# Laying a kernel's spare path ahead of its main path, and regrouping its mixer: one change of a tuned transformer block

## The chip, the cores and the metric

The kernel runs on one core of a Trainium2 chip. The metric is the device time of one execution in microseconds (us), lower is better; the figure quoted for a kernel is the median of its runs. Five engines appear: PE (matmul; PEld is its weight load), ACT (activations), DVE (vector work), POOL (general work), SP (used here only to issue DMAs).

## The reference, cut to what matters

```python
mod = (silu(c) @ w_mod).reshape(1, 6, 1, 640)        # c: (1, 640), w_mod: (640, 3840)
sa, ca, ga, sb, cb, gb = (mod[:, i] for i in range(6))
h = layernorm(x) * (1 + ca) + sa                     # x: (2048, 640), bfloat16
q = h @ wq                                           # 32 heads of 128
o = softmax(q @ k_cache.T * 128**-0.5) @ v_cache     # caches: 32 x 2048 x 128
x = x + ga * (o @ wo)                                # modulation 2 is ga
h = layernorm(x) * (1 + cb) + sb
# the mixer: u = gelu(layernorm(h) @ w1); four groups of 160 channels are shifted by
# 1, -1, 2, -2 rows; x1 = h + u_shifted @ w2; then an MLP of width 1728
x = x + gb * (x1 + gelu(layernorm(x1) @ w3) @ w4)
```

Of the kernel before, what the change touches and what calls it, by code (L numbers as in the profile page):

```python
# [6 lines left out]
ACT = mybir.ActivationFunctionType  # L7
# [33 lines left out]
class Plan:  # L41
# [3 lines left out]
    ENG = ("PE", "ACT", "DVE", "POOL", "SP")  # L45

# [115 lines left out]
    def emit(self, nc, es, ndma, redo, flag):  # L162
        hint = {}
# [67 lines left out]
        def body(e):  # L231
            def f(eng):
                for i, o in enumerate(self.seq[e]):
                    if e == "PE" and i == len(self.seq[e]) - 300:
                        hint[e] = eng.mark_branch_hint_location()
                    for sem, v in waits[o].items():
                        eng.wait_ge(sem, v)
                    ins = o.fn(eng)
                    if o.dma:
                        ins.then_inc(o.sem, 16)  # L240
                    elif o.needed:
                        ins.then_inc(o.sem, 1)
                eng.wait_ge(self.flag_op.sem, self.flag_op.semval)
                eng.load(redo[eng.engine], flag[0:1, 0:1])
                for sem in dsem.get(e, ()):
                    if fin.get(sem, 0) > know[e].get(sem, 0):
                        eng.wait_ge(sem, fin[sem])
            return f

        block = es.enter_context(nc.Block())  # L250
        block.tensor(body("PE"))
        block.scalar(body("ACT"))
        block.vector(body("DVE"))
        block.gpsimd(body("POOL"))
        block.sync(body("SP"))
        return hint


def fast_path(nc, es, flag, A_x, A_k_cache, A_v_cache, A_wq, A_wo, B_w1, B_w2, B_w3, B_w4, c, w_mod, out):
# [72 lines left out]
    us = [T() for _ in range(NC)]  # L332
# [16 lines left out]
    W12 = [T(), T()]  # L349
    w_half = [W12_t[:, i * KT * D:(i + 1) * KT * D].rearrange("p (k n) -> p k n", k=KT) for i in range(2)]  # L350
# [23 lines left out]
    def dma(eng, fn, kb, reads, writes, prio, need=()):  # L374
        return P.op(eng, fn, {"SP": 480, "ACT": 480, "POOL": 1000}[eng], reads, writes, prio, dma=True, kb=kb, need=need)
# [9 lines left out]
    for i in range(NKV):  # L385
        P.op("POOL", lambda e, i=i: e.memset(V_ap[i][:, :, 128:130], 1.0), 200, (), (V[i],), -297 + i)
# [16 lines left out]
    x0 = load_x2(0, -301) + load_x2(2, -301, eng="ACT")  # L403
# [29 lines left out]
    P.op("DVE", lambda e: e.tensor_copy(s_bc.ap, c_f.ap.unsqueeze(2).to_broadcast([128, KT, 128])), 800, (c_f,), (s_bc,), 0.5)  # L433
    spin(50, -298)
    for k in range(KT):
        def mcol(e, k=k):
            for j in range(2 * KT):
                ins = e.matmul(mc[:, j:j + 1], wm_ap[:, k, j * 128:(j + 1) * 128], s_bf[:, k:k + 1],
                               start=(k == 0 and j == 0), stop=(k == KT - 1), skip_group_check=True)
                if k < KT - 1:  # L440
                    dummy(e, 1)
            return ins
        P.op("PE", mcol, 2 * KT * 120, (wm[k], s_bf, ones), (mc,) + ((warm,) if k < KT - 1 else ()), -290 + k, accum=True)
    spin(12, -281)
# [83 lines left out]
    def ln1(ch, prio):  # L528
        g = ln_slot()
        xs = x0 if ch == 0 else load_x2(4 * ch, XP[ch], from_slot(XS[ch])) + load_x2(4 * ch + 2, XP[ch], from_slot(XS[ch]))  # L530
        for a in (0, 2):
            for i in (a, a + 1):
                ln_stats(xs[i].ap, (xs[i],), g, i, prio, 0.0 if ch == 0 else 2000.0)
            rstd_act(g, a, a + 2, prio - 100)
# [3 lines left out]
        if ch == 0:  # L538
# [5 lines left out]
            for i in range(4):  # L544
# [4 lines left out]
                P.op("PE", tr, 330, (xn[i], ident), (hp[0], hp[1], hq, hp[4]), -280 + i, accum=True)  # L549
                spin(6 if i < 3 else 10, -279.5 + i)  # L550
# [18 lines left out]
    def load_k(h, prio, gate=(), need=()):  # L569
        b = h % NKV  # L570
        for i in range(4):
            dmaT(lambda e, i=i: e.dma_start_transpose(K_ap[b][:, i * 512:(i + 1) * 512].unsqueeze(1), A_k_cache[0, h, i * 512:(i + 1) * 512, :]),
                 128, gate, (K[b][i],), prio + 0.01 * i, need)
# [5 lines left out]
    def load_wq(g, a, b, prio, need=()):  # L579
        dma("SP", lambda e: e.dma_start(wq_t[g % 2][:, :, a * 128:b * 128],  # L580
                                        A_wq[:, (g * HG + a) * 128:(g * HG + b) * 128].rearrange("(k p) d -> p k d", p=128)),
            160 * (b - a), (), tuple(wq[g % 2][a:b]), prio, need)
# [8 lines left out]
    load_k(0, -296)  # L591
    load_v(0, -290, "ACT", gate=(wm[3],))
    ln1(0, -280)

    def load_head(h):
# [3 lines left out]
        load_k(h, pr, need=from_slot(n))  # L599
        load_v(h, pr + 1, need=from_slot(n + 1))  # L600
# [6 lines left out]
    load_wq(0, 1, HG, -295)  # L607
# [4 lines left out]


    MS = 17
    for n, p in enumerate((2, 4, 3, 5)):
        dma("SP", lambda e, n=n, p=p: e.dma_start(w_half[n % 2], w_mod[:, p * D:(p + 1) * D].rearrange("(k p) n -> p k n", p=128)),
            800, (), (W12[n % 2],) + (tuple(wm) if n < 2 else ()), MS * NP - 30 + n, from_slot((MS + 2 * n) * NP - 20))
        for hf in range(2):
            m = Tile(pool="M")
            sl = slice(hf * HD, (hf + 1) * HD)  # L620
            for k in range(KT):
                i = (n * 2 + hf) * KT + k
                P.op("PE", lambda e, m=m, sl=sl, k=k, n=n: e.matmul(m[:, 0:HD], s_bc[:, k, :], w_half[n % 2][:, k, sl], start=(k == 0), stop=(k == KT - 1)),
                     MM(HD), (s_bc, W12[n % 2]), (m,), NP * (MS + i // KT) + 4 + i % KT + 0.65, accum=True)
            P.op("DVE", lambda e, m=m, p=p, hf=hf: e.tensor_scalar_add(out=mod[p][hf].ap, in0=m[:, 0:HD], scalar1=1.0 if p == 4 else 0.0),
                 490, (m,), (mod[p][hf],), NP * MS - 60)

# [1045 lines left out]
```

## The kernel before: what the change and the argument touch

The program is a list of operations, each with tiles that it reads and writes and a priority. A scheduler fixes the order on each engine ahead of time, and `emit` writes the five instruction streams with semaphore waits. Attention is 128 "steps": 32 heads in eight groups of four, by four chunks of 512 queries. A step has eight pairs of score matmuls, eight exponentials of 1024 columns on ACT, and the matmuls with V. `TAIL` is the order of the pieces of mixer and MLP: A = `w1`, B = `w2`, C = `w3`, D = `w4`, WO = the last output projection.

The main path skips the maximum of the softmax. At the end it computes a flag from the row sums; if the flag is set, a general path computes everything again. **With these inputs the general path never runs**, but its code lies in the program.

```python
# emit, before: one block, a body for each engine; a barrier closes the block
def body(e):
    def f(eng):
        for i, o in enumerate(self.seq[e]):
            if e == "PE" and i == len(self.seq[e]) - 300:
                hint[e] = eng.mark_branch_hint_location()
            ...                                    # waits, the instruction, its increments
        eng.wait_ge(self.flag_op.sem, self.flag_op.semval)
        eng.load(redo[eng.engine], flag[0:1, 0:1])
        ...
# launch, before: then each engine jumps, over the general path, to "done"
for e, eng in nc.engines.items():
    br = eng.br_cmp(redo[e], 0, comp_op="IS_EQ", on_true="done", on_false="general")
    if eng is nc.tensor:
        br.branch_hint(hint["PE"])
with nc.body("general"):
    general_path(nc, ...)
    nc.br("done")
nc.switch_bb("done")
```

The start: `spin(n)` is n dummy matmuls which keep PE busy; `mcol` makes the first two modulations (sa, ca), in five pieces as their weights `wm[k]` arrive.

```python
x0 = load_x2(0, -301) + load_x2(2, -301, eng="ACT")
... # wm[k]: five loads of 320 KB on SP and ACT;  spin(30);  silu(c);  spin(50);  mcol x 5
spin(12, -281)
... # chunk 0: layer norm; for each of four row tiles:
    P.op("PE", tr, 330, (xn[i], ident), (hp[0], hp[1], hq, hp[4]), -280 + i, accum=True)   # transposes
    spin(6 if i < 3 else 10, -279.5 + i)
... # hT[0] = transposes * ca + sa (ACT and DVE);  first query projection;  spin(8)
for n, p in enumerate((2, 4, 3, 5)):               # the other modulations, in steps 17 to 24
    dma("SP", ...)                                 # 800 KB each
    for hf in range(2): ...                        # 5 matmuls of 320 columns each
```

The end of an attention step, on DVE, and the second layer norm:

```python
evac.append(P.op("DVE", lambda e, ...: e.tensor_tensor(          # O out of its bank, divided by the row sums
    out=On_ap[gs][:, 2 * bk:2 * bk + 2, hh, :], in0=ov[...], in1=rl_t[...], op=ALU.mult), 430, ...))

def rstd_dve(g, a, b, prio):                                     # [128 x 2] values, Newton steps
    for ca, cb in ((-0.703952253, 1.68191391), (-0.5, 1.5)):
        D_(lambda e, ca=ca: e.scalar_tensor_tensor(out=t, in0=r, scalar=ca, in1=r, ...), ...)
        D_(lambda e: e.tensor_tensor(out=t, in0=t, in1=v, op=ALU.mult), ...)
        D_(lambda e, cb=cb: e.scalar_tensor_tensor(out=r, in0=t, scalar=cb, in1=r, ...), ...)

def mlp_in(ch, prio):                                            # before the mixer
    eng = "DVE" if tail else "POOL"                              # tail: the last chunk, 3
    ...   # statistics (DVE), 1/sqrt (ACT, DVE in the tail), three passes on eng, statistics, one more pass
```

## Time and profile before

| | before |
|---|---|
| time, median of the first 3 runs | 1400.83 us (1400.35 to 1401.3) |
| run that was profiled | 1400.4 us; its span in the trace 1394.5 us |
| first softmax exponential of step 0 | 17.19 us from the span's start |
| first matmul of the mixer | 1205.69 us |
| last matmul ends | 1389.95 us |

The span is what the trace records of the engines' work; the reported time is 5.9 us longer. From the page of the profile before: the span, the busy time of each engine, and the chain of work that ended last.

```profile
span 1394.5 us, 29726 instructions
PE 1367.3 (98%) x12941; PEld 943.8 (68%) x13176; DVE 518.6 (37%) x1337; ACT 1125.9 (81%) x1195; POOL 123.8 (9%) x106
PE 96%; ACT 2%; issue 1%; DVE 0%; DMA 0%; POOL 0%; ACTq 0%; POOLq 0%
```

PE sets the time. So only PE's waits, its dummies, its slow stretches and the two ends can be gained. PE's waits, as "waiting line <- what released it: us in total, times, longest":

```profile
PE f_S L668 <- ACT f_PQ L836: 3.3, 1, 3.3
PE f_S L712 <- ACT f_PQ L714: 2.2, 3, 1.3
PE f_S L850 <- ACT f_PQ L836: 0.8, 1, 0.8
```

The first is the passage from attention to mixer: the last projection (L668) waits for a bank that GELUs (L836) on ACT have to empty. The second is mostly in step 0. The same passage as a table of stretches, the clock that PE was granted being the PEclk column:

```profile
core 0: us, PE busy (x) PEld busy (x) DVE busy (x) ACT busy (x) POOL busy (x), PEclk, DMA share, GB/s
1211.00:1214.29 3.29, 0.04 (x2) 0.04 (x2) 0.00 (x0) 3.21 (x6) 3.15 (x3) 1.00 0.87 170
1214.29:1217.60 3.31, 2.88 (x14) 1.56 (x14) 1.55 (x3) 3.22 (x6) 1.62 (x2) 0.71 0.25 50
1217.60:1221.00 3.40, 3.40 (x21) 2.27 (x20) 2.68 (x6) 0.91 (x1) 0.00 (x0) 0.78 0.01 2
```

PE does nothing for 3.29 us and then works at a lower clock: the trace records half clock from 1215.66 to 1219.07. Last, the start as ACT's timeline shows it: start, duration, engine (ACTq: its queue issues a DMA), what it did.

```profile
4.46 0.18 ACT L428 ACTIVATE f_small<-f_M 128x5 f32<-128x5 f32 x1 [0.99 <-PE f_M L424]
7.71 0.41 ACTq L577 DMA_DIRECT2D f_KV<-in_A_v_cache_dram  x1
8.45 0.20 ACT L477 ACTIVATE f_small<-f_small 128x2 f32<-128x2 f32 x1 [3.81 <-DVE f_small L473]
13.64 0.78 ACT L553 ACTIVATE f_hT<-f_O,f_small 128x512 bf16<-128x512 bf16 x1 [2.85 <-PE f_M L547]
```

ACT's layer-norm work (L477) starts at 8.45 when DVE's statistics are there, and hT, the input of the first query projection, at 13.64.

### The profile page before, as it was taken

How to read it: one execution, taken by the hardware profiler on the slowest of the kernel's cores; microseconds unless marked ns; L12 is line 12 of the kernel's file. 1: busy time of each engine (PE TensorE's matmuls, PEld its weight loads, DVE VectorE, ACT ScalarE, POOL GpSimd, SP SyncE). 2: the span in 40 equal slices, each digit the busy share in tenths (PEclk: the TensorE clock that was granted, in tenths of full speed). 3: DMA queues.
4: the chain of work that ended last, by engine and by line, in shares of the span. 5: the costliest groups of instructions: out<-in, count | busy, mean ns of one | idle time of the engine just before them, and what ended most of it. 6: DMA issues, size and time to landing. Idle time of an engine off the chain costs nothing.

```text
span 1394.5 us, 29726 instructions
## 1 busy us (share of the span) xinstructions
PE 1367.3 (98%) x12941; PEld 943.8 (68%) x13176; DVE 518.6 (37%) x1337; ACT 1125.9 (81%) x1195; POOL 123.8 (9%) x106
## 2 busy tenths in 40 slices
PE   8999999999999999999999999999999999899998
PEld 6667776776777777777776777777777666555554
DVE  5453323233323332233323332333223345585552
ACT  5988888888888889888888888888988888864222
POOL 0000000000000000000000000001233376600000
PEclk9999999999999999999999999999999999999999
DMA  9652623261215221241115112612353112411210
GB/s 204 128 107 38 136 57 86 49 107 35 47 35 88 54 47 35 58 84 39 43 24 99 32 39 31 107 35 47 54 107 98 17 36 51 111 39 48 34 39 24
DMA packets 258963, 88.82 MB, mean 64 GB/s; under 512 B 236625, under 2 KB 257554, under 8 KB 258834
## 3 DMA queue, kind: packets, MB, share of 16 engines
q1 hardware_dynamic: 256210, 85.41, 30.9%
q8 instruction: 104, 1.70, 0.5%
q10 hardware_dynamic: 2624, 1.51, 0.5%
q14 instruction: 25, 0.20, 0.1%
HBM read 43.48 MB, written 2.62 MB: 33 GB/s over the span
## 4 chain that ended last, share of the span: by engine, by line
PE 96%; ACT 2%; issue 1%; DVE 0%; DMA 0%; POOL 0%; ACTq 0%; POOLq 0%
PE f_O L731 34%; PE f_S L712 29%; PE f_M L643 10%; PE f_M L668 10%; PE f_S L890 2%; PE f_M L890 2%; PE f_S L877 2%; PE f_O L877 2%; ACT f_PQ L714 1%; PE f_S L850 1%; PE f_M L850 1%; PE f_S L413 1%; PE f_S L832 1%; ACT f_PQ L836 1%; PE f_O L832 0%
## 5 line engine op out<-in xcount | busy, mean ns | idle before, releaser
L714 ACT ACTIVATE f_PQ<-f_S 128x1024 bf16<-128x1024 f32 x1024 | 1041.5, 1024 | 143.5 <-PE f_S L712 106.4
L731 PEld LDWEIGHTS f_O<-f_KV,f_PQ 128*128 128x128 bf16 x8192 | 593.7, 98 | 231.9 <-ACT f_PQ L714 0.5
L731 PE MATMUL f_O<-f_KV,f_PQ 128*128 128x129 bf16 x8192 | 720.2, 220 | 7.8 <-ACT f_PQ L714 0.3
L712 PE MATMUL f_S<-f_PQ,f_KV 128*128 128x512 bf16 x1856 | 671.3, 379 | 5.3 <-ACT f_PQ L714 2.2
L676 DVE TENSOR_TENSOR f_y<-f_M,f_y 128x320 f32<-128x320 f32 x192 | 94.4, 492 | 524.1 <-PE f_M L668 524.1
L668 PE MATMUL f_M<-f_wo,f_OO 128*128 128x320 bf16 x992 | 270.2, 299 | 0.0
L712 PEld LDWEIGHTS f_S<-f_PQ,f_KV 128*128 128x128 bf16 x2048 | 196.2, 97 | 34.4 <-ACT f_PQ L714 3.9
L643 PE MATMUL f_M<-f_hT,f_wq 128*128 128x512 bf16 x608 | 170.8, 379 | 2.2 <-DVE f_hT L557 0.5
L511 POOL TENSOR_TENSOR f_y<-f_y,f_mod 128x640 f32<-128x640 f32 x40 | 61.4, 1542 | 1056.9 <-DVE f_y L676 1049.5
L668 PEld LDWEIGHTS f_M<-f_wo,f_OO 128*128 128x128 bf16 x992 | 95.1, 98 | 27.9
L740 DVE TENSOR_TENSOR f_OO<-f_O,f_rl 128x256 bf16<-128x256 f32 x256 | 108.4, 423 | 8.3
L646 DVE CAST f_PQ<-f_M 128x512 bf16<-128x512 f32 x128 | 88.5, 691 | 54.3 <-PE f_M L643 53.7
L643 PEld LDWEIGHTS f_M<-f_hT,f_wq 128*128 128x128 bf16 x640 | 62.3, 98 | 62.9 <-DVE f_hT L557 1.0
L738 DVE RECIPROCAL f_rl<-f_O 128x2 f32<-128x2 f32 x256 | 43.5, 170 | 47.2 <-PE f_O L731 42.9
L880 ACT ACTIVATE f_OO<-f_O 128x512 bf16<-128x512 f32 (+1 forms) x28 | 16.7, 596 | 36.2 <-PE f_O L877 36.1
L674 DVE COPY f_y<-f_M 128x320 f32<-128x320 f32 x32 | 15.7, 490 | 67.4 <-PE f_M L668 67.4
L880 ACT ACTIVATE f_OO<-f_S 128x512 bf16<-128x512 f32 (+1 forms) x28 | 16.7, 596 | 27.5 <-PE f_S L877 27.5
L890 PE MATMUL f_S<-f_KV,f_OO 128*128 128x320 bf16 x224 | 34.3, 300 | 0.0
L890 PE MATMUL f_M<-f_KV,f_OO 128*128 128x320 bf16 x224 | 34.3, 300 | 0.0
L472 DVE BATCH_NORM_STATS2 f_small<-f_y 128x6 f32<-128x320 f32 x64 | 29.3, 478 | 7.9 <-POOL f_y L511 7.9
L890 PEld LDWEIGHTS f_M<-f_KV,f_OO 128*128 128x128 bf16 x224 | 20.6, 97 | 14.0 <-issue 5.5
L890 PEld LDWEIGHTS f_S<-f_KV,f_OO 128*128 128x128 bf16 x224 | 20.5, 97 | 13.3 <-issue 4.2
(119 smaller groups left out, 517.4 us busy)
## 6 DMA issues: line engine op xcount, KB each, us to landing
f_KV<-in_A_v_cache_dram SPq DMA_DIRECT2D x31, 512.0 KB, 4.9
f_wo<-in_A_wo_dram SPq DMA_DIRECT2D x8, 640.0 KB, 4.3
f_xin<-in_A_x_dram SPq DMA_DIRECT2D x15, 320.0 KB, 3.8
f_wq<-in_A_wq_dram SPq DMA_DIRECT2D x7, 640.0 KB, 4.5
f_W<-in_w_mod_dram SPq DMA_DIRECT2D x4, 800.0 KB, 4.8
out_dram<-f_xin SPq DMA_DIRECT2D x16, 160.0 KB, 1.8
f_KV<-in_B_w_dram SPq DMA_DIRECT2D x5, 432.0 KB, 3.5
f_KV<-in_A_k_cache_dram SPq DMA_TRANSPOSE x128, 2.8
```

The source lines that it names most:

```text
L511: P.op(eng, lambda e: e.tensor_tensor(out=out, in0=a, in1=b, op=op), COST[eng][0], rd, wr, prio, lat=300 if eng == "POOL" else None)
L643: P.op("PE", lambda e, i=i, kk=kk: e.matmul(m.ap, wq_t[g % 2][:, kk, hh * 128:(hh + 1) * 128], hT_t[ch][:, kk, :], start=(i == 0), stop=(i ...
L646: P.op("DVE", lambda e: e.tensor_copy(q.ap, m.ap), 690, (m,), (q,), s * NP - 90)
L668: P.op("PE", lambda e, m=m, qt=qt, hf=hf, hh=hh: e.matmul(m[:, 0:HD], OT_ap[gs][:, qt, hh, :], wo_t[g % 2][:, hh, hf * HD:(hf + 1) * HD], ...
L676: P.op("DVE", lambda e, m=m, yt=yt: e.tensor_tensor(out=yt.ap, in0=m[:, 0:HD], in1=yt.ap, op=ALU.add), 490, (m, yt), (yt,), s * NP - 60)
L712: P.op("PE", lambda e, sp=sp, r=r, kt=kt: e.matmul(sp[:, r * QC:(r + 1) * QC], K_ap[b][:, kt * 128:(kt + 1) * 128], q.ap, start=True, stop ...
L714: x = P.op("ACT", lambda e, sp=sp, pt=pt: e.activation(pt.ap.rearrange("p k q -> p (k q)"), sp.ap, ACT.Exp, scale=SCALE), 1021, (sp,), (pt ...
L731: ins = e.matmul(o[bk][:, w * 129:w * 129 + 129], pt[:, r, qt * 128:(qt + 1) * 128], V_ap[b][:, u, 0:129], start=(u == 0 and w == 0), stop ...
L738: P.op("DVE", lambda e, ov=ov, i0=i0: e.reciprocal(rl_t[:, i0:i0 + 2].unsqueeze(2), ov[:, 0:258].rearrange("p (u d) -> p u d", u=2)[:, :, ...
L740: evac.append(P.op("DVE", lambda e, ov=ov, i0=i0, bk=bk: e.tensor_tensor(out=On_ap[gs][:, 2 * bk:2 * bk + 2, hh, :], in0=ov[:, 0:258].rear ...
L877: P.op("PE", lambda e, m=m, f=f, kk=kk, fs=fs: e.matmul(m[0:fs, :], w3_ap[:, kk, f * 128:f * 128 + fs], nT_ap[ch][:, kk, :], start=(kk == ...
L890: P.op("PE", lambda e, f=f, hf=hf, fs=fs: e.matmul(m[:, hf * 512:hf * 512 + HD], gT_ap[0:fs, f, i * 128:(i + 1) * 128], w4_ap[f][0:fs, hf ...
```

## The change

Six things are meant to shorten the ends and the passage.

1. *Layout.* The streams go straight into the program: a few first operations, a hinted jump over the general path to "fast", the general path, the main path, and "done" right behind it. No block, so no barrier at its end.
2. *Modulation 2 early.* Its 800 KB come in the first 15 us through a free K/V buffer, and its matmuls leave steps 17 and 18.
3. *Shorter start.* The dummies between transposes go, the broadcast moves from DVE to POOL, some loads get a gate so that they don't go ahead of the first ones.
4. *Mixer channels regrouped.* Four blocks of 128 channels, one for each shift, plus one block of the 4 x 32 remaining ones: five GELUs per chunk in place of nine pieces, and four copies on DVE.
5. *Normalisation of chunk 2.* Its late half goes from POOL and ACT to DVE, as does the sum of its output projection, and the order of the pieces (`TAIL`) changes.
6. *Last row tile in halves,* so that its first half is stored while PE still works.

```diff
+    FIRST = {"PE": 3, "ACT": 5, "DVE": 0, "POOL": 7, "SP": 7}
...
-        block = es.enter_context(nc.Block())
-        block.tensor(body("PE"))            # ... and so on for five engines
+        for e, eng in names.items():
+            hint = eng.mark_branch_hint_location()
+            run(e, 0, self.FIRST[e])
+            eng.br("fast").branch_hint(hint)
+        es.close()
+        general()
+        nc.switch_bb("fast")
+        for e, eng in names.items():
+            run(e, self.FIRST[e], None)
+            ...                              # flag, last waits
+        for e, eng in names.items():
+            eng.br_cmp(redo[eng.engine], 0, comp_op="IS_EQ", on_true="done", on_false="general")
+        nc.switch_bb("done", parent=first)
...  # start
-    x0 = load_x2(0, -301) + load_x2(2, -301, eng="ACT")
+    x0 = load_x2(0, -301, eng="ACT") + load_x2(2, -301)
-    spin(12, -281)
-                spin(6 if i < 3 else 10, -279.5 + i)
-            spin(8, -260)
...  # loads of the first heads: gates
-    load_wq(0, 1, HG, -295)
+    load_wq(0, 1, HG, -295.985, gate=(wm[2],))
...  # modulations
-    for n, p in enumerate((2, 4, 3, 5)):
+    for n, p in enumerate((4, 3, 5)):        # 2 is made near the first query cast, from a 800 KB load on ACT
...  # the passage
-    TAIL = ("A0 WO B0 B1 B2 A1 B3 A2 B4 B5 B6 B7 C0 I3 D0 D1 D2 D3 C1 A3 ...
+    TAIL = ("A0 B0 B1 B2 A1 B3 WO B4 B5 A2 B6 I3 B7 B8 C0 B9 D0 D1 D2 D3 C1 ...
+            pool = ch < NC - 2 or (ch == NC - 2 and a == 0)
+                if pool: ...                 # as before
+                else:
+                    rstd_dve(g, a, a + 2, prio)     # and two passes on DVE in place of three on POOL
...  # w1: one GELU per 128 channels; the last 4 x 32 channels by way of DVE copies
-            for (p0, p1, dl) in segs[n]:
-                P.op("ACT", ... us_ap[p0:p1, n, ...], m[p0:p1, :], GELU ...)
+            if n == 4: ...                   # GELU to a spare tile, four copies of 32 rows on DVE
+            else: P.op("ACT", ... us_ap[:, n, c0:c0 + QC], m.ap, GELU ...)
...  # w4, last tile: DVE twice 320 columns and a store for each half
```

## The prediction

> **What bounds the kernel.** PE is busy 98% of the 1394.5 us span (page, part 1); the chain of waits is 96% PE; from 30 to 1195 us the list of PE's waits is empty. A 512-column matmul costs about 0.216 us, a 320-column one 0.136. The change removes no matmul but dummies, so it gains only where PE waits, runs dummies or runs slowly: the first 28 us, the passage from attention to mixer (1205 to 1245 us), and both ends. The time is 6 us longer than the span (1400.4 against 1394.5): some start or end work is outside the records.
>
> **Terms, in us.**
>
> 1. Passage, -6.5. From 1205.7 to 1245 PE does 75 x 0.216 + 112 x 0.136 = 31.4 of work in 39.3. The 7.9 lost are 3.25 idle ahead of the last projection (for GELUs on ACT), 0.43, 0.81, 0.83 and 0.21 of other idle, and a granted clock of 0.71 to 0.78 after the long gap (table of stretches): 32 projection matmuls took 6.7 in place of 4.35. ACT pays nine GELU pieces of 0.6 per chunk and seven table loads of 1.28. Regrouped, a chunk has five GELUs and four copies on DVE; the late half of chunk 2's normalisation goes to DVE, so most table switches vanish; the projection moves behind B3 while its transposes land. I leave 1.4 of new short waits (B0 and B3 behind their last GELU; DVE gets more work).
>
> 2. Modulation 2, -1.4. Ten 320-column matmuls leave PE-bound steps for PE's idle around the first query cast (0.70 and 0.34 idle at 15.8 and 17.2). Their 800 KB load joins the crowded first 15 us; I expect it in time, near 13.
>
> 3. First chunk, -1.4. The dummies between transposes (6, 6, 6, 12 of 0.056) and the broadcast on DVE (0.80 at 8.69) leave the path; transposes 0 and 1 go ahead of the last modulation piece. The first hT operation should start near 12.3, not 13.65.
>
> 4. ACT's wait from 22.4 to 23.9 for DVE's statistics, which costs PE 1.33 at 25.05: the new slack moves those small ACT operations later. -1.2.
>
> 5. Last tile in halves: after the last matmul 0.49 + 0.49 on DVE, not 0.82 + 0.82. -0.7.
>
> 6. Outside the records, -2.7. The block's barrier goes, and "done" follows the main path directly; before, four engines jump unhinted over the whole general path. [...] the term is a guess bounded by the 6 us. The new jump at the start should cost little: PE has dummies until 7.3, DVE's first operation was at 4.67.
>
> Sum about -14. The last group's projections only change place; I count nothing.
>
> **Prediction: 1386 us, 80% range 1379 to 1393.** Faster by over 2% (below 1372.8): 2%; within 2%: 97%; slower: 1%.
>
> **Signs:** PE's waits after 1200 (no 3 us one, granted clock 1.0 throughout); one or two table loads on ACT after 1206; first hT operation near 12.3; no 1.3 us PE wait near 25; steps 17 to 24 shorter by 1.4 in all; time minus span 3 to 4 us.
>
> **What would make it wrong:** the extra 800 KB delaying K, V or the modulation, so that PE waits in the first 20 us; DVE becoming the limit between B3 and C0; a jump that stalls an engine at the start (DVE goes first); the 6 us being fixed cost, which leaves about 1389.

The sum stands: -6.5 - 1.4 - 1.4 - 1.2 - 0.7 - 2.7 = -13.9, the "about -14".

## The result, and the profile after

The kernel after took **1397.2 us** (median of 4 runs, 1396.16 to 1397.48) against 1400.59 (1399.84 to 1401.3) for the kernel before in the same rounds. The ratio is 0.9975, with a 95% interval of 0.9957 to 0.9992. A ratio here is the mean time of one kernel's fast runs over that of the other's in the same rounds, so it is not quite the ratio of the medians quoted. The prediction, 1386 with a range of 1379 to 1393, was wrong: the change gained 3.4 us and not 14.

The stretches of the two profiled runs (1400.40 and 1397.48 us), beside what the terms of the prediction put there. "First exponential" is the first 1024-column exponential of a step.

| stretch | before | after | difference | predicted |
|---|---|---|---|---|
| start to first exponential of step 0 | 17.19 | 20.96 | +3.77 | -1.4 |
| step 0 | 9.88 | 8.31 | -1.57 | -1.2 |
| steps 1 to 8 | 69.80 | 71.81 | +2.01 | 0 |
| steps 9 to 29 | 199.75 | 198.39 | -1.36 | -1.4 |
| steps 30 to 126 | 900.32 | 900.79 | +0.47 | 0 |
| step 127 to the first mixer matmul | 8.75 | 8.42 | -0.33 | 0 |
| first mixer matmul to last matmul's end | 184.26 | 184.65 | +0.39 | -6.5 |
| last matmul's end to the reported end | 10.45 | 4.15 | -6.30 | -3.4 |
| sum | 1400.40 | 1397.48 | -2.92 | -13.9 |

Three rows miss badly: the start is longer, the passage gains nothing, and the end gains nearly twice what was said. The page of the profile after, the same three lines. (Its PE total is not comparable: the trace before lacks some 2% of the matmul records.)

```profile
span 1396.2 us, 29870 instructions
PE 1382.3 (99%) x13128; PEld 942.0 (67%) x13128; DVE 539.8 (39%) x1380; ACT 1106.6 (79%) x1164; POOL 110.4 (8%) x96
PE 97%; DVE 2%; issue 1%; DMA 0%; SPq 0%; ACT 0%; ACTq 0%; POOL 0%; POOLq 0%
```

ACT's 3.3 us wait is gone from PE's list; a DVE wait of 3.7 has come in its place, and small ones at the start:

```profile
PE f_O L857 <- DVE f_OO L755: 3.7, 1, 3.7
PE f_O L553 <- DVE f_xn L510: 1.5, 2, 0.9
PE f_O L746 <- DMA f_KV<-in_A_v_cache_dram: 0.5, 1, 0.5
```

The start of the kernel after, ACT's timeline:

```profile
4.70 0.18 ACT L435 ACTIVATE f_small<-f_M 128x5 f32<-128x5 f32 x1
10.68 0.38 ACTq L612 DMA_DIRECT2D f_KV<-in_w_mod_dram  x1
11.69 0.20 ACT L483 ACTIVATE f_small<-f_small 128x2 f32<-128x2 f32 x1 [6.81 <-issue]
15.80 0.78 ACT L558 ACTIVATE f_hT<-f_O,f_small 128x512 bf16<-128x512 bf16 x1 [1.65 <-PE f_M L553]
20.96 1.02 ACT L729 ACTIVATE f_PQ<-f_S 128x1024 bf16<-128x1024 f32 x1 [3.72 <-PE f_S L727]
```

Read the bracket of the third line: 6.81 us idle, "<-issue", so nothing that the profile shows held ACT back; before, the same operation stood at 8.45. The clue lies in the raw records of the trace, where the jumps are instructions of their own (us from the span's start):

```
engine  hint at  jump recorded at  next instruction at
ACT     0.73     4.71              10.68  (the load it waits for landed at 6.61)
SP      0.73     6.96              14.04  (the one it waits for had landed at 9.96)
DVE     0.76     0.85               4.91  (when its operand came)
POOL    0.69     1.43               1.62
```

On both engines 4.1 us pass between the landing of the awaited load and the next instruction, so the new gates alone do not explain the stall.

Part of the passage after, in stretches of PE's wait and of the slow clock behind it (half clock from 1213.15 to 1219.97):

```profile
1211.00:1214.75 3.75, 0.00 (x1) 0.00 (x1) 3.54 (x15) 0.60 (x1) 0.00 (x0) 0.79 0.00 0
1214.75:1218.00 3.25, 3.25 (x8) 1.19 (x9) 3.25 (x13) 0.60 (x1) 0.00 (x0) 0.50 0.40 81
1218.00:1220.50 2.50, 2.50 (x8) 0.95 (x7) 0.87 (x4) 0.60 (x1) 0.00 (x0) 0.61 0.65 92
```

And DVE and POOL ahead of that wait:

```profile
1203.42 6.04 POOL L517 TENSOR_TENSOR f_y<-f_y,f_mod 128x640 f32<-128x640 f32 x4
1203.49 1.48 DVE L496 SCALAR_TENSOR_TENSOR f_small<-f_small 128x2 f32<-128x2 f32 x1
1205.01 1.47 DVE L497 TENSOR_TENSOR f_small<-f_small 128x2 f32<-128x2 f32 x1
1206.51 1.47 DVE L498 SCALAR_TENSOR_TENSOR f_small<-f_small 128x2 f32<-128x2 f32 x1
1208.01 2.92 DVE L794 SCALAR_TENSOR_TENSOR f_y<-f_y,f_small,f_mod 128x640 f32<-128x640 f32 x2
1213.60 0.16 DVE L497 TENSOR_TENSOR f_small<-f_small 128x2 f32<-128x2 f32 x1
1214.27 0.42 DVE L755 TENSOR_TENSOR f_OO<-f_O,f_rl 128x256 bf16<-128x256 f32 x1
1215.26 0.37 DVE L755 TENSOR_TENSOR f_OO<-f_O,f_rl 128x256 bf16<-128x256 f32 x1
```

Two values per partition take 1.47 us while POOL runs its four multiplies of 1.51, and 0.16 once POOL is done. Meanwhile the last two O banks (L755) stay full until 1214.27 and 1215.26. Before, the same two operations came as soon as the banks were ready:

```profile
1205.65 0.42 DVE L740 TENSOR_TENSOR f_OO<-f_O,f_rl 128x256 bf16<-128x256 f32 x1
1206.32 0.42 DVE L740 TENSOR_TENSOR f_OO<-f_O,f_rl 128x256 bf16<-128x256 f32 x1
```

### The profile page after: what moved, and what is told of

Read it like the earlier page. It is cut to its first block, busy times and chain, and to the rows that moved or that the text cites. A ratio compares the mean times of both kernels' runs of the same rounds, so it can differ in the third digit from the quotient of the medians.

```text
span 1396.2 us, 29870 instructions
## 1 busy us (share of the span) xinstructions
PE 1382.3 (99%) x13128; PEld 942.0 (67%) x13128; DVE 539.8 (39%) x1380; ACT 1106.6 (79%) x1164; POOL 110.4 (8%) x96
## 4 chain that ended last, share of the span: by engine, by line
PE 97%; DVE 2%; issue 1%; DMA 0%; SPq 0%; ACT 0%; ACTq 0%; POOL 0%; POOLq 0%
PE f_O L746 33%; PE f_S L727 31%; PE f_M L659 10%; PE f_M L684 10%; PE f_M L921 3%; PE f_O L907 2%; PE f_S L907 2%; PE f_S L921 2%; PE f_S L880 1%; PE f_O L857 1%; PE f_S L857 1%; PE f_M L880 1%; DMA f_KV<-in_A_v_cache_dram 0%; PE f_M L604 0%; PE f_S L420 0%
## 5 line engine op out<-in xcount | busy, mean ns | idle before, releaser
L727 PE MATMUL f_S<-f_PQ,f_KV 128*128 128x512 bf16 x2048 | 727.9, 380 | 0.5 <-ACT f_PQ L729 0.5
L684 PE MATMUL f_M<-f_wo,f_OO 128*128 128x320 bf16 x992 | 273.3, 300 | 0.0
L659 PE MATMUL f_M<-f_hT,f_wq 128*128 128x512 bf16 x640 | 177.4, 381 | 1.1 <-DVE f_hT L562 0.6
L517 POOL TENSOR_TENSOR f_y<-f_y,f_mod 128x640 f32<-128x640 f32 x36 | 55.6, 1557 | 820.1 <-DVE f_y L692 819.9
L755 DVE TENSOR_TENSOR f_OO<-f_O,f_rl 128x256 bf16<-128x256 f32 x256 | 108.5, 424 | 8.2
L910 ACT ACTIVATE f_OO<-f_S 128x512 bf16<-128x512 f32 x28 | 16.7, 597 | 39.6 <-PE f_S L907 39.6
L921 PE MATMUL f_M<-f_KV,f_OO 128*128 128x320 bf16 x252 | 38.6, 301 | 0.0
L523 ACT ACTIVATE f_xn<-f_y,f_small 128x640 bf16<-128x640 f32 x10 | 9.1, 914 | 29.6 <-DVE f_small L502 29.6
L921 PE MATMUL f_S<-f_KV,f_OO 128*128 128x320 bf16 x196 | 30.0, 301 | 0.0
```

Source lines behind the costliest of these rows:

```text
L517: P.op(eng, lambda e: e.tensor_tensor(out=out, in0=a, in1=b, op=op), COST[eng][0], rd, wr, prio, lat=300 if eng == "POOL" else None)
L659: P.op("PE", lambda e, i=i, kk=kk: e.matmul(m.ap, wq_t[g % 2][:, kk, hh * 128:(hh + 1) * 128], hT_t[ch][:, kk, :], start=(i == 0), stop=(i ...
L684: P.op("PE", lambda e, m=m, qt=qt, hf=hf, hh=hh: e.matmul(m[:, 0:HD], OT_ap[gs][:, qt, hh, :], wo_t[g % 2][:, hh, hf * HD:(hf + 1) * HD], ...
L727: P.op("PE", lambda e, sp=sp, r=r, kt=kt: e.matmul(sp[:, r * QC:(r + 1) * QC], K_ap[b][:, kt * 128:(kt + 1) * 128], q.ap, start=True, stop ...
L755: evac.append(P.op("DVE", lambda e, ov=ov, i0=i0, bk=bk: e.tensor_tensor(out=On_ap[gs][:, 2 * bk:2 * bk + 2, hh, :], in0=ov[:, 0:258].rear ...
L921: P.op("PE", lambda e, f=f, hf=hf, fs=fs: e.matmul(m[:, hf * 512:hf * 512 + HD], gT_ap[0:fs, f, i * 128:(i + 1) * 128], w4_ap[f][0:fs, hf ...
```

## The experiments

Theory at this point: (a) the jump at the start costs ACT and SP several us, which the end pays back; (b) the passage is held by DVE, whose small operations take 1.47 us in place of 0.16 beside POOL's multiplies. Rivals: the early 800 KB load, the gates or the dropped dummies slow the start, and the jump is innocent. Every kernel below gave correct results. "Ratio" is to the kernel before in the same rounds. Two readings recur: the start of step 0 and of step 9 (first exponentials; before, 17.19 and 96.87) in the profiled run. Those are one run each, and runs of one kernel scatter by 1 to 6 us, so a milestone is used for *where* time goes and the ratio of the four or five runs for *how much*. A measure of that scatter: in d_nomod2, f_dve and f_evac the order of work on ACT, DVE, POOL and SP is the same for the first 400 us, and step 9 stands at 95.40, 98.49 and 95.07. The experiments ran on five chips; only runs that share their rounds share a chip (a and b; c; d; f; g).

| run | what it is | median us | ratio [95%] | step 0 | step 9 |
|---|---|---|---|---|---|
| b_layout | before + layout | 1403.06 | 1.0020 [1.0006, 1.0033] | 19.91 | 104.36 |
| a_straight | after - layout | 1400.99 | 0.9997 [0.9983, 1.0011] | 16.81 | 99.39 |
| a_late | after, jump near 100 us | 1395.57 | 0.9965 [0.9951, 0.9978] | 17.97 | 101.54 |
| a_pool2 | after, chunk 2 on POOL | 1394.3 | 0.9964 [0.9950, 0.9977] | 22.08 | 100.62 |
| c_tail | after, jump at the end | 1394.45 | 0.9967 [0.9954, 0.9981] | 17.39 | 98.77 |
| c_tail_pool2 | c_tail + chunk 2 on POOL | 1393.15 | 0.9946 [0.9933, 0.9960] | 19.12 | 98.73 |
| c_nogate | c_tail_pool2 - gates | 1395.82 | 0.9967 [0.9953, 0.9981] | 19.20 | 102.91 |
| c_nomod2 | c_nogate - early load | 1392.97 | 0.9947 [0.9934, 0.9961] | 21.68 | 99.88 |
| d_before | before + layout, jumps at the end | 1395.42 | 0.9965 [0.9952, 0.9979] | 17.07 | 97.15 |
| d_tail | c_tail_pool2, PE's jump late too | 1394.74 | 0.9952 [0.9938, 0.9966] | 16.38 | 101.49 |
| d_nogate | d_tail - gates | 1397.84 | 0.9981 [0.9967, 0.9994] | 16.35 | 102.89 |
| d_nomod2 | d_nogate - early load | 1393.11 | 0.9954 [0.9940, 0.9967] | 16.59 | 95.40 |
| f_spins | after + dummies | 1397.3 | 0.9983 [0.9969, 0.9997] | 20.08 | 101.95 |
| f_gate | d_tail - early load, gates kept | 1392.34 | 0.9950 [0.9936, 0.9964] | 16.45 | 96.17 |
| f_dve | d_nomod2, chunk 2 on DVE | 1393.63 | 0.9949 [0.9936, 0.9963] | 16.76 | 98.49 |
| f_evac | f_dve, evacuations first | **1391.71** | 0.9944 [0.9931, 0.9958] | 16.29 | 95.07 |
| g_first0 | after, ACT and SP jump first of all | 1401.05 | 1.0002 [0.9986, 1.0019] | 28.40 | 106.89 |

### First four: which part of the change does what

**b_layout** gives the kernel before the new `emit` and launch, and nothing else; **a_straight** gives the kernel after the old ones.

```diff
 b_layout = before.py
-    emit (block, body, barrier) and launch of before
+    emit (FIRST, hinted jump) and launch of after
```

> The kernel before with the new layout alone (jump at the start, general path ahead, no barrier, nothing else). Theory: the jump is what delays the start (in the changed kernel ACT's next instruction came 5.9 us after its jump and SP's 7.0, with their semaphores long up), so the first softmax exponential starts 2 to 4 us later than before's 17.19, while the end outside the span shrinks from 5.9 to about 1.3 us and the barrier's 0.8 goes: the time is 1396 to 1399. Rival: the new gates, the 800 KB load and the missing dummies delay the start and the jump is free: the exponential starts at 17.2 and the time is 1395.0 to 1395.5 (5.4 saved at the end).

```diff
 a_straight = after.py
-    emit and launch of after
+    emit and launch of before
```

> The changed kernel with the layout of before (no jump at the start, barrier and general path at the end). Theory: the first exponential starts near 16 instead of 20.96, PE stays at full clock in the first 25 us, and the time outside the span is 5.9 again: 1397.2 - 4.5 + 5.4 = about 1398 (1396.5 to 1399.5). Rival (gates, load, dummies): the first exponential stays near 20.5 and the time is about 1402.5.

The layout alone makes the kernel *slower*: 1403.06 against 1400.14, where 1396 to 1399 was expected. It has none of the new gates, and SP's next instruction still comes 7.06 us after its jump. It loses 2.7 us up to step 0 and 7.5 up to step 9; in step 0 the trace shows PE waiting 1.2 us for query weights and 3.1 us for an exponential, while ACT waits 3.3 us for DVE's statistics. It gains 4.8 at the end (last matmul to reported end: 5.64, not 10.45). Without the layout, a_straight starts step 0 earlier than the kernel before. But its time, 1400.99, missed the expected 1396.5 to 1399.5: at a ratio of 0.9997 the other five parts together, as built, are worth nothing that can be measured. ACT's timeline in a_straight:

```profile
5.72 0.39 ACTq L609 DMA_DIRECT2D f_KV<-in_w_mod_dram  x1
8.02 0.20 ACT L480 ACTIVATE f_small<-f_small 128x2 f32<-128x2 f32 x1 [3.21 <-DVE f_small L476]
13.27 0.78 ACT L555 ACTIVATE f_hT<-f_O,f_small 128x512 bf16<-128x512 bf16 x1 [2.63 <-PE f_M L550]
```

The load that came out of ACT's queue at 10.68 in the kernel after comes at 5.72 here; the layer norm stands at 8.02, not at 11.69. So theory (a) stands for the time up to step 0: 20.96 against 16.81. But a_straight is at step 9 only at 99.39, 2.5 behind the kernel before, without any jump. That is a second loss, and (a) doesn't explain it.

**a_late** moves the jumps of ACT, DVE and SP to 100 to 116 us, where these engines were thought to have slack, and POOL's to 19, with the hints 12 operations ahead. **a_pool2** gives chunk 2 back to POOL.

```diff
 a_late
-    FIRST = {"PE": 3, "ACT": 5, "DVE": 0, "POOL": 7, "SP": 7}
+    FIRST = {"PE": 3, "ACT": 110, "DVE": 144, "POOL": 9, "SP": 61}     # hint 12 operations ahead
```

> The changed kernel with the jump moved to a calm time: ACT after 110 operations, DVE 144, SP 61, POOL 9 (about 100 us in), the hint 12 operations ahead; PE as it is. Theory: the start is as in the straight one (first exponential near 16) and the end stays short: about 1392.5 (1391 to 1394). If a jump in mid-run costs ACT its 6 us, which PE cannot absorb there, a new PE wait of 2 to 4 us shows near 100 us and the time is 1394 to 1397. Rival (gates, load, dummies): 1397.

```diff
 a_pool2
-            pool = ch < NC - 2 or (ch == NC - 2 and a == 0)
+            pool = ch < NC - 1
```

> The changed kernel with the late half of chunk 2's normalisation back on POOL. Theory: the DVE operations with two SBUF inputs that took 1.47 us in place of 0.15 between 1203 and 1208 were waiting for POOL, and being ahead of the last evacuation of the O banks in DVE's order they caused PE's 3.75 us wait at 1211 and the half clock after it. With them gone that wait vanishes and PE's clock stays 1.0: 4 to 6 us saved, unless the table switches and POOL's later chain open a wait at A2 (up to 3 us): 1391.5 to 1396. Rival (DVE has simply too much work): DVE's last evacuation is still 4 us late and the time stays within 1 us of 1397.

a_late: step 0 at 17.97, 3 us earlier than after, though steps 9 to 29 are now 1.4 us longer (a new 1.3 us wait of the scores for an exponential just behind ACT's jump), and step 9 is as late as in after. a_pool2: the 3.7 us wait and the half clock in the passage are both gone, and the stretch from first mixer matmul to last matmul is 181.36 in place of 184.65. So (b) stands for the wait: DVE's late half of chunk 2 brought it. But even this passage is 2.9 shorter than before's, not 6.5, and most of its lead over the kernel after is clock: c_tail below has the same passage as the kernel after, with the wait and without the half clock, and takes 181.87.

### Jumps at the very end, and the start's second loss

In **c_tail** the jumps of four engines come late, a few operations before their end (POOL's at 1219.65, the others at 1339 to 1359 of 1391). PE keeps its early one. The next three take away one more part each.

```diff
 c_tail
-    FIRST = {"PE": 3, "ACT": 5, "DVE": 0, "POOL": 7, "SP": 7}
+    LAST = {"PE": None, "ACT": 14, "DVE": 12, "POOL": 0, "SP": 5}      # jump so many operations before the end
 c_tail_pool2 = c_tail, and
+            pool = ch < NC - 1
 c_nogate = c_tail_pool2, and
-    load_wq(0, 1, HG, -295.985, gate=(wm[2],))   # likewise the gates of K and V of heads 0 and 1
+    load_wq(0, 1, HG, -295)
 c_nomod2 = c_nogate, and
-    for n, p in enumerate((4, 3, 5)):            # and the early load of modulation 2
+    for n, p in enumerate((2, 4, 3, 5)):
```

> The changed kernel with the jump of ACT, DVE, SP and POOL moved to the last 40 us of the kernel, where they idle (ACT 14 operations before its end, DVE 12, SP 5, POOL behind its last); PE jumps early as in the change. Theory: the start is that of the straight layout (first hT operation near 13.3, first exponential near 16.8) and the end that of the change (about 1.3 us outside the span, no barrier): profiled time 1401.4 - 5.4 = 1396 (1394.5 to 1397). Rival: a jump costs its 6 us wherever it stands; then PE waits in the last 40 us for a GELU or an output bank, and the time is 1398 to 1402.

> The same, and the late half of chunk 2's normalisation on POOL. Theory: the two add up: passage from the first mixer matmul to the last matmul 181.4 in place of 184.7, so about 1393 (1391.5 to 1394.5). If they interact (the start's delay hid part of the passage's), 1394.5 to 1396.

> c_tail_pool2 without the new gates of K's, V's and wq's first loads on the third modulation piece. Theory: SP's queue is busy without a break for the first 46 us (26 DMA transposes of 1.26 us each and more), the gate makes it stand 2.2 us, and V of the fourth head lands at 47.4 in place of 44.0, which costs PE 2.3 us and a half clock near 48. Without the gate SP issues that V near 40, PE's wait for it vanishes, and the time is 2 to 3 below c_tail_pool2, about 1390.5. Rival (the 800 KB of early traffic, not the gate): the wait stays at 2 us and the time within 0.7 of c_tail_pool2.

> c_nogate with modulation 2 back in steps 17 and 18, so without the early 800 KB. If the early load costs nothing once the gate is gone: 1.4 slower than c_nogate. If the load itself is what makes the first heads late: the start gains 1 to 3 us, and the time is equal to c_nogate or up to 1.5 below it.

c_tail: 1394.45, where the kernel after had 1397.2; that was on another chip, and the intervals of the ratios, 0.9967 and 0.9975, overlap. It has the 3.8 us DVE wait but in its profiled run no half clock behind it, and so does 16 matmuls behind the wait where the kernel after did 8:

```profile
1208.69:1212.44 3.75, 0.00 (x0) 0.00 (x1) 3.54 (x15) 0.60 (x1) 0.00 (x0) 1.00 0.01 2
1212.44:1215.70 3.26, 3.26 (x16) 1.49 (x17) 3.25 (x13) 1.20 (x2) 0.00 (x0) 1.00 0.41 83
```

c_tail_pool2 gains a further 1.3 in the median, with intervals that overlap too. c_nogate is *slower* than c_tail_pool2 by 2.7, each of its runs slower than each of the other's: my theory that the gates caused the second loss fell here. c_nomod2 gets 2.9 back by leaving the early load out. These four keep PE's early jump, and the traces show PE idle for "issue" behind it, 3.3 us in the profiled run of c_nomod2. That blurs step 0 (17.39 to 21.68), so the series was done again with PE's jump at the end as well, and once on the kernel before.

```diff
 d_before = b_layout, and
+    LAST = {"PE": 100, "ACT": 14, "DVE": 10, "POOL": 0, "SP": 4}       # PE's hint 60 operations ahead
 d_tail, d_nogate, d_nomod2 = c_tail_pool2, c_nogate, c_nomod2, and
+    LAST = {"PE": 100, "ACT": 14, "DVE": 12, "POOL": 0, "SP": 5}
```

> The kernel before with the general path laid out ahead and no barrier, all five jumps in the last 40 us (PE 100 matmuls before its end, its hint 60 matmuls earlier). Theory: the start is untouched (first exponential 17.2, ninth step 96.9) and the end loses the 4.6 us outside the span and the barrier's 0.8: 1400.4 - 5.4 = 1395.0 (1394.3 to 1395.7). Rival: PE's jump stands for 1 to 3 us in the middle of the last output tiles: 1396 to 1398.

> c_tail_pool2 with PE's jump moved to the end as well. Theory: PE's early jump is what is left of the jump's cost at the start (PE idle for 0.9 to 3.3 us at issue behind it, half clock from 15 us, one of SP's issues of 1.6 in place of 0.45): without it the first exponential is at 16.8 as in the straight layout, the runs scatter less, and the time is 1390.5 to 1393. Rival: those are ordinary scatter of the loads, and it stays at 1393.

> d_tail without the gates on the first K, V and wq loads. c_nogate was 2.7 slower than c_tail_pool2, against my theory of SP's 2.2 us stand; if that holds without PE's jump in the way, the gates help once the early 800 KB are there, and this is 1.5 to 3.5 slower than d_tail (a wait for wq of the second head, later hT of chunk 1). If c_nogate's loss was PE's jump and scatter, this is within 1 of d_tail.

> d_nogate without the early modulation 2 (it goes back to steps 17 and 18), so loads as in the kernel before except for x's queues. If the early load is what makes the first heads late, the ninth step starts at 95 to 96.5 (before 96.87, minus 1.2 for ACT's wait and what the first chunk gains) in place of 98.7 to 99.4, and the time is d_tail plus 1.4 minus 2.5 to 3.5: 1 to 2 below d_tail. If the load is harmless, it is 1.4 above d_tail.

**d_before is the cleanest result.** The kernel before with the layout and with late jumps runs in 1395.42 against 1400.56: 5.1 us for the end alone, with nothing lost at the start (step 0 at 17.07, before 17.19). Its last matmul ends 5.37 us before the reported end, not 10.45. The same layout with the jump at the start had cost 2.9 (1403.06 against 1400.14). And d_before's ratio, 0.9965 [0.9952, 0.9979], overlaps that of every kernel here that has other parts of the change and late jumps. The medians of the best of them are 2 to 4 us lower, but beyond the layout no gain of the rest is shown by the intervals.

d_tail missed its expectation at step 9: step 0 came at 16.38 as hoped, but step 9 only at 101.49. Its list of PE's waits up to 60 us is headed by V of the fourth head:

```profile
PE f_O L750 <- DMA f_KV<-in_A_v_cache_dram: 3.3, 1, 3.3
```

That V landed at 49.5 us, having been issued at 43.56; in the kernel before it was issued at 39.41 and landed at 43.98. In a_straight it landed at 47.4. SP's queue stands 3.4 us at the new gate, from 5.7, and has next to no pause from there to 46 us; twelve of its 20 transposing loads take 1.26 to 1.28 us each, the slowest 3.3. With early load and no gates (d_nogate) that V is issued at 40.05 and lands at 44.73, in time, and PE waits for something else, query weights and hT:

```profile
PE f_M L663 <- DVE f_hT L573: 4.0, 3, 3.0
PE f_M L663 <- DMA f_wq<-in_A_wq_dram: 2.6, 1, 2.6
```

Without the early load (d_nomod2) the wait for V is 0.9 and step 9 stands at 95.40, earlier than before. By the ratios: leaving the load out turns 0.9981 into 0.9954 with late jumps, and 0.9967 into 0.9947 with PE's early one. The two intervals of the first pair only touch; those of the second overlap. While the early load is there, the gates help: each run of d_tail is faster than each of d_nogate (medians 1394.74 and 1397.84), as with c_tail_pool2 and c_nogate.

### What the start still leaves, and the passage with DVE

```diff
 f_spins = after, and
+    spin(14, -286.7)          # and spin(12), spin(10), spin(8) near the places they had before
 f_gate = d_tail, and
-    for n, p in enumerate((4, 3, 5)):            # without the early load of modulation 2; the gates stay
+    for n, p in enumerate((2, 4, 3, 5)):
 f_dve = d_nomod2, and
-            pool = ch < NC - 1
+            pool = ch < NC - 2 or (ch == NC - 2 and a == 0)
 f_evac = f_dve, and
-        D_(lambda e: e.tensor_scalar_add(out=v, ...), tuple(mvs[g][a:b]), (v_,))
+        D_(lambda e: e.tensor_scalar_add(out=v, ...), tuple(mvs[g][a:b]), (v_,), after)   # after = evac[-2:]
-                        825, (x1[t], mvs[g1][i]) + tuple(mod[4]), (xb[t],), prio)
+                        825, (x1[t], mvs[g1][i]) + tuple(mod[4]), (xb[t],), prio, after=tuple(evac[-2:]))
```

> The changed kernel with the dummies put back (14 ahead of transpose 0, 12 ahead of transpose 2, 10 behind transpose 3, 8 behind the first query projection). Theory: the 6.8 us of half clock from 15.07, in which the first projection took 2.34 us in place of 1.24 and the modulation and the first scores ran half as fast, came from PE standing idle while ACT hung in its jump; with the dummies the clock stays full and the first exponential starts 1.5 to 2.5 us earlier (18.5 to 19.5), time about 1395.5. Rival: the loads set the start (V of head 0, K), so that a warm PE only waits longer, and step 9 starts at 101 as before, time 1397. If the dummies are too few for the gaps, the half clock stays and the run tells nothing.

> d_nomod2 with the gates on K, V and wq kept: the loads' gates without the early 800 KB. d_nomod2's ninth step began at 95.4, d_tail's (gates and load) at 101.5, d_nogate's (load, no gates) at 102.9. If the load is the cause, this is at 95 to 97 and the time within 1.5 of d_nomod2's 1393.1. If the gates cost on their own, 98 or later and 1395 to 1397.

> d_nomod2 with the changed kernel's passage (late half of chunk 2 on DVE). Theory: DVE's two-input operations wait for POOL again, the last O evacuation comes 4 us late, PE waits 3.7 us near 1205 and, where that wait is followed by half clock, loses 1.7 to 3.4 more: 0.5 to 3.5 slower than d_nomod2 (1393.6 to 1396.5).

> f_dve with DVE's normalisation of chunk 2's late half ordered behind the last evacuation of the O banks. Theory [...]: PE's 3.7 us wait behind the evacuation is gone. What DVE is late with then comes later: the plan's own model puts a 4.9 us wait at the last projection (its evacuations stand behind the normalisation), so the time is not better than f_dve, 1395 to 1399, with the wait at the projection and no longer at the first mixer matmuls. Rival (the evacuation is late for another reason): the 3.7 us wait stays where it was.

**f_spins.** The kernel after has PE at half clock from 15.07 to 21.89, so the dropped dummies were suspect. With dummies back the clock stayed full there, and yet nothing was gained: 1397.3, step 9 at 101.95. V of the fourth head was waited for 2.2 us, and half clock followed at 51 instead. The half clock of the start was a mark of the delay, not its cause.

**f_gate.** Gates kept, load gone: step 9 at 96.17, 1392.34. So the gates alone cost nothing that the times show. By time, f_gate and d_tail cannot be told apart (0.9950 and 0.9952, with intervals over each other): with gates, the cost of the early load is shown only by the 5 us between two traces at step 9, where the same code was seen to scatter by 3.4, and d_tail's profiled run was the slowest of its five. Nor is the wait for V the early load's alone: without that load it is still 0.9 us in d_nomod2 and f_evac, 1.8 in f_gate and 2.1 in f_dve.

**f_dve and f_evac** show what carries the wait in the passage. f_dve has chunk 2's late half on DVE, as the kernel after, its small operations again take 1.48, 1.47 and 1.47 us (from 1202.26), and the wait is back:

```profile
PE f_O L856 <- DVE f_OO L754: 3.8, 1, 3.8
```

f_evac keeps all of DVE's work and changes its order only: the late half of chunk 2 comes behind the two O evacuations. DVE's timeline in f_evac (on POOL, the four multiplies had ended by 1204.8):

```profile
1204.16 0.42 DVE L754 TENSOR_TENSOR f_OO<-f_O,f_rl 128x256 bf16<-128x256 f32 x1
1205.15 0.37 DVE L754 TENSOR_TENSOR f_OO<-f_O,f_rl 128x256 bf16<-128x256 f32 x1
1208.63 0.16 DVE L500 SCALAR_TENSOR_TENSOR f_small<-f_small 128x2 f32<-128x2 f32 x1
1209.13 0.16 DVE L501 TENSOR_TENSOR f_small<-f_small 128x2 f32<-128x2 f32 x1
```

The O banks are emptied from 1204.16 and 1205.15 on, and the small operations, now behind POOL's multiplies, take 0.16 in place of 1.47. The 3.8 us wait is gone. (POOL does not slow all of DVE: the evacuation at 1204.16, with its large input from a matmul bank, takes its usual 0.42 while a multiply runs; in the kernel after, 43 evacuations lie beside POOL's multiplies, with the same median of 0.42 us as the 209 that lie outside them.) A new one has come at the last projection, because chunk 2 is now late on DVE:

```profile
PE f_O L683 <- DVE f_small L502: 2.7, 1, 2.7
```

So the passage (182.90 from first mixer matmul to last matmul) gains 1.4 of the 6.5 predicted, with one stretch of half clock behind the new wait. In f_dve's profiled run it is even shorter, 181.87, because there no half clock followed the wait of 3.8. Over the whole kernel f_evac has the lowest median, 1391.71 (1391.27 to 1395.47), against 1400.66 for the kernel before, where I had expected 1395 to 1399; each of its runs is faster than every run of the kernel after (1396.16 at best), though not on the same chip. f_dve's interval overlaps f_evac's, so the order alone is not shown to gain by time, and neither is the choice of engine (f_dve and d_nomod2: 0.9949 and 0.9954); that the order removes the wait is shown by the trace.

### Is the jump slow because loads are in the way?

ACT's jump took 5.97 us to the next instruction, with loads under way: the mean busy share of the 16 DMA engines stayed at 0.7 or more until 9.9 us. One theory: what the jump waits for stands behind those loads; then a jump before the first load costs little. The rival: the jump takes some us anyway. **g_first0** lets ACT and SP jump before they issue anything.

```diff
 g_first0
-    FIRST = {"PE": 3, "ACT": 5, "DVE": 0, "POOL": 7, "SP": 7}
+    FIRST = {"PE": 3, "ACT": 0, "DVE": 0, "POOL": 7, "SP": 0}
```

> The changed kernel with ACT and SP jumping before their first operation (0 in place of 5 and 7), [...]. This measures the disputed cost by itself. Theory [...]: the stall of ACT and SP falls from 6 to 7 us to 1.5 to 3, their first loads are issued at 2.5 to 4 us in place of 0.8, the first exponential starts at 18.5 to 20 in place of 20.96, and the time is 1394.5 to 1397. Rival (a jump of these engines costs some 6 us whatever else moves): first loads at about 6.8, first exponential at 22.5 or later, 1398 to 1401.

ACT jumps at 0.80 and issues its first load at 4.05; SP jumps at 0.84 and issues at 4.65: 3.3 and 3.8 us with no load of the kernel in the way. And the first issue itself takes 2.2 and 2.5 us, where the same two took 0.42 and 0.35 in the kernel after. In g_first0:

```profile
4.05 2.20 ACTq L405 DMA_DIRECT2D f_xin<-in_A_x_dram  x1
4.65 2.47 SPq L409 DMA_DIRECT2D f_xn<-in_c_dram  x1
PE f_M L431 <- DMA f_xn<-in_c_dram: 5.5, 1, 5.5
```

PE then waits 5.5 us for c, and the kernel is no faster than before: 1401.05. By time and first exponential (28.40) the rival was nearer; by the stall itself neither was right, as 3.3 and 3.8 lie between the theory's 1.5 to 3 and the rival's 6. The jump cost 3.3 and 3.8 us there by itself, and the 5.97 and 7.1 us of the kernel after are that and more. The first 8192-byte packet on the instruction queues behind ACT's jump also starts later, 3.2 us after it in the kernel after (7.89), and 0.9 us in g_first0 (1.73). The trace doesn't say which engine a packet is for: that ACT waited for these packets is not shown, nor whether loads or other packets were in the way.

## Why the prediction was wrong, point by point

**"The new jump at the start should cost little" failed.** This step turned a gain of 1.4 into a loss of 3.77; b_layout and a_straight put 2.7 to 4.2 us up to step 0 on the layout alone. The prediction looked at PE, which had dummies until 7.3 us, and at DVE, whose first operation stood at 4.67. DVE did have that slack: its next instruction came at 4.91, with its operand. ACT and SP had none: between 4.7 and 14 us they issue the loads for K, V and query weights, and ACT computes the layer norm. The same text counted the jumps over the general path at the end as a cost, worth 2.7 us to drop with the barrier (term 6), and a jump over the same path at the start as next to nothing. The traces show 5.97 us from jump to next instruction on ACT and 7.1 on SP, 3.3 and 3.8 in g_first0. The records of the jumps themselves are short: in the kernel after 47 to 69 ns for the first, unconditional ones (PE's 344) and 50 to 75 for the last, conditional ones (PE's 93); so the time passes behind them. The hints, 4.0 us (ACT) and 6.2 us (SP) ahead of those two jumps, did not hide it; POOL's next instruction came 0.19 us after its jump.

**Term 3, "first hT operation near 12.3", was right in direction, too large, and covered by the jump.** It came at 15.80 with the jump, and without it at 13.27 (a_straight) and 12.75 (f_evac). Step 0 then stood at 16.81 and 16.29, where 17.19 less 1.4 is 15.8: a quarter to two thirds of the term.

**Term 2, -1.4 for modulation 2, was right for steps 9 to 29 (-1.36), and its other half failed.** Those steps take 198.39 in a_straight and c_tail, and 199.75 again in d_nomod2 and f_gate, where the matmuls are back in their old place. "I expect it in time, near 13" asked whether that load itself comes in time, and not what it and the gates set around it push back. With both, V of the fourth head, which PE needs in step 3, landed 3.4 us (a_straight) and 5.5 us (d_tail) later than before; with the load and no gates (d_nogate) V came in time, and query weights and hT were late. Steps 1 to 8 were 2.0 us longer in the kernel after; f_gate, without the load, has the same 2.0, so these are not shown to be the load's. The waits listed there name 0.5 for V, 0.6 for O banks and 0.2 for hT of the next chunk; the remaining 0.7 I can't place. The prediction did name "the extra 800 KB delaying K, V" as a risk, but only for the first 20 us; it hit at 48.

**Term 4, -1.2 for ACT's wait, was right for step 0:** it is 1.57 shorter and the 1.3 us wait of PE near 25 us is gone. Not all of it stays: even without the early load (d_nomod2, f_evac) steps 1 to 8 are 1.0 longer, as PE now comes to V of the fourth head 0.9 us too early.

**Term 1, the passage at -6.5, failed: +0.39.** ACT's side went much as said: four table loads after 1206 us, where there were seven (the prediction named one or two), and no wait for GELUs above 0.4. But the work went to DVE with only "DVE gets more work" set against it, in an allowance of 1.4. Two things were missed. In DVE's list the late half of chunk 2 stood ahead of the O evacuations that PE's next bank needs: DVE worked on it from 1203.49, and the last two evacuations came at 1214.27 and 1215.26. And the small operations were taken as short, while POOL was running its multiplies. The trace shows three operations on 256 values of 1.48, 1.47 and 1.47 us while POOL ran multiplies of 1.51, about the length of one multiply each, and 0.16 for the same lines after it.

The wait of 3.75 was followed by 6.8 us of half clock. That clock cost more than the wait: with the same wait and no half clock the passage gained 2.4 (c_tail, f_dve), and with chunk 2 on POOL and no half clock 2.9 to 3.1 (a_pool2, c_nomod2). So the term was too big besides: of PE's 5.5 us of gaps in the first 42 us of the passage it left 1.4, and the traces show 4.8 in the kernel after and 3.6 and 3.8 in a_pool2 and c_nomod2, where three waits of 0.8 to 0.9 for DVE have come.

**Term 5, -0.7 for the last tile in halves, was right:** a_straight, which has the halves and not the layout, takes 9.60 from the last matmul to the reported end in place of 10.45, so -0.85.

**Term 6, -2.7 outside the records, was right in direction and half of what came.** The layout is worth 5.1 in d_before, and in the kernel after 9.60 - 4.15 = 5.45 beside a_straight. In the kernel before, the trace shows packets of 8192 bytes on the instruction queues from 1394.9 us, behind the final jumps at 1393.9 to 1394.3, and more until 1399.6; in the kernel after the last is at 1333.88, long before the end. Of the 5.9 us outside the span 4.6 went with it (1.33 remain, in d_before too), and the span itself lost 0.5 (d_before) to 1.3 us (after beside a_straight) behind the last matmul, in part the barrier (SP's two last jumps in the kernel before, ahead of it and behind it, stand at 1393.57 and 1394.33). The prediction took the 5.9 as a bound and guessed half; most of it went.

**Granted clock "1.0 throughout" failed,** as the wait failed. The clock records of the traces before and after have three slow stretches up to the last matmul, each at 0.5 of full clock: 3.41 us before (from 1215.66), 6.83 and 6.83 us after (from 15.07 and from 1213.15). The length of a wait does not tell what clock follows: in the kernel after 3.75 us of waiting brought 6.8 us of half clock, in c_tail and f_dve the same wait of 3.8 brought none. Shorter waits had half clock behind them too, 2.7 us in f_evac and 2.2 in f_spins, and in d_nomod2 two of 0.8 and 0.95 within 3.2 us, while the same two in a_pool2 had none. What decides it the runs do not show. Some of the 1 to 6 us between runs of one kernel goes with the granted clock: c_tail's two fastest runs (1392.62, 1393.21) have a granted clock of 1.000 and 0.999, its two slowest (1397.37, 1398.29) 0.996, and 0.004 of 1392 us is 5.6 by estimate. It is not so everywhere: c_nomod2 has 1392.48 and 1394.96 at the same clock of 0.997.

In sum, by the stretches of the two profiled runs: terms 4 and 5 and the gain in steps 9 to 29 came (-3.8 together) and the layout gave twice its guess (-5.45); the start took 5.8 of that back (3.77 up to step 0, 2.01 in steps 1 to 8), and the passage gave nothing. The two failures are of one kind: I costed an operation by its own length and its own deadline, and not by what stood behind it in its engine's list: the jump in ACT's and SP's, the gate in SP's, the normalisation in DVE's.

What stays open: what a jump's 3 to 7 us on ACT and SP consist of, and why POOL's hinted jump was free and ACT's and SP's were not; how the loss up to step 9 in the kernel after divides between jump, gates and early load, since they overlap; and whether with gates the early load costs anything in the mean.

## What to carry to other kernels

Put a jump over unused code where the engine that takes it has slack, which ACT and SP, with the first loads to issue, did not have at the start here (3.3 to 7.1 us from jump to next instruction), and jump at the end if the layout is to be kept: here that was worth 5.1 us, against a loss of 2.9 with the jump at the start. Before work is moved to an engine that "has time", list what is already queued on it just behind the new place and who waits for that; then order the urgent operation first. When an early load is added, ask which later load in the same queue moves back, and look for its reader well after the start.
